# Filler matmuls in the setup of an attention and gated-MLP kernel, and a one-hot permute moved to ScalarE

## The chip, the cores and the metric

The kernel runs on one core of a Trainium2 chip. A core has five engines with instruction queues of their own: PE (TensorE, matrix products; its weight loads are listed apart as PEld), DVE (VectorE), ACT (ScalarE), POOL (GpSimd) and SP (SyncE, which here only issues transfers). Matmul results go to a small accumulation memory, PSUM, operands lie in SBUF, inputs and outputs in HBM, which DMA queues move. The metric is the device time of one execution in microseconds (us); smaller is better. The profile gives besides the span, from the first to the last instruction, and the clock that was granted to PE as a share of its full speed.

## The reference

Block-sparse attention over 4 batches of 8 heads, 768 positions of 64 dimensions, then a gated MLP whose gate mixes positions. A position block of 32 sees its neighbours, the first and last block, and three sampled blocks per row, which are an input.

```python
scores = scale * np.matmul(q, k.transpose(0, 1, 3, 2))
mask = np.abs(blk_i - blk_j) <= window
mask = mask | (blk_i == 0) | (blk_j == 0) | (blk_i == n_blocks - 1) | (blk_j == n_blocks - 1)
for qb in range(n_blocks):
    for kb in sampled_blocks[qb]:
        mask[qb * block:(qb + 1) * block, kb * block:(kb + 1) * block] = True
scores = np.where(mask, scores, -1000000000.0)
attn = softmax(scores)            # written out in the reference
x = (attn @ v), heads side by side: [4, 768, 512]

h = np.maximum(x @ w_in, 0.0)
u, v = halves of h
v_n = (v - mu) / np.sqrt(var + 1e-06)
v_s = np.einsum('ts,bsd->btd', w_spatial, v_n) + b_spatial[None, :, None]
out = (u * v_s) @ w_out
```

## The kernel before

The 32 (batch, head) units are walked in 16 pairs. The order of all instructions is written out by hand; the engines take theirs in program order, and a wait stops everything behind it on the same engine.

**The mask as extra rows.** The mask is not applied to the scores. Each key tile `kt` and query tile `qt` has 64 rows of data and 24 more: `kt` has the one-hot rows of the block of each position (`ind`), `qt` has the product of `bm` (0 where a block pair is allowed, a negative constant where it is not) with `ind`. So one matmul over 88 rows gives masked scores. `ind_nat` is made by POOL in natural order of positions (L157); `ind` is the same with the positions permuted to the order in which the data lies on the partitions (position 6p + c goes to column c*128 + p), a copy on POOL at L160.

**Setup.** SP and ACT issue the first loads: head 0 and head 1 of q and k in halves, then the rest. PE runs eight matmuls of 512 columns on a zero tile `warm` into a PSUM tile `wps` (L143 to L145) that nobody reads. DVE builds `allowed` from the sampled blocks with three operations (L172), then `bm` (L176), casts query head 0 (`nat_q`, L109), copies `ind` into `kt[0]` (L180). ACT casts key head 0 (`nat_k`, L107). Then PE transposes the keys (`tr_head`, L191, six transposes to PSUM), multiplies the mask rows (`mq`, L208), and transposes the queries (L191 again). DVE copies the transposed keys and queries out of PSUM (L183), ACT copies `mq` into `qt[0]` (L186). With that the first score tile can run.

**The main loop.** A step g handles one of the six 128-row key tiles of one head, 12 steps to a pair p. In a step, in this order: `qk_exp` (two score matmuls, L244, into one of two `sc` PSUM buffers, then one exponential on ACT, L248), in the first pairs preparation of later pairs, pieces of the MLP of an earlier batch, and, 7 steps behind, `av` (six matmuls against the values, L260), after six of which `norm` divides (L273, L274). For p = 0 there are also the copies of the mask rows to the other tiles (`mask_rows`, L215 and L216), head 1 of the pair (`second_head`, and `tr_head(1, ...)` at steps 3 and 4).

Pairs 1 to 4 are transposed on PE (`tr_pair`, L199); later ones by a transposing DMA on SP's queue (`tr_dma`, L227) out of the bf16 tiles that POOL casts (`prepare`, L109 and L112), and split by DVE (`split_pair`, L233). From pair 4 on the MLP of the batch before (L332 to L403) is spread over 48 steps; the last batch's MLP follows the loop. The attention output of every fourth pair is transposed on PE (`xtr`, L283), of the others by DMA (L287).

PSUM has four kinds of tiles, two buffers each where given: `moe` (transposes and MLP), `sc` (scores), `av` (value products).

Of the kernel before, what the change touches and what calls it, by code (L numbers as in the profile page):

```python
# [10 lines left out]
FP32 = mybir.dt.float32  # L11
BF16 = mybir.dt.bfloat16
I32 = mybir.dt.int32
AF = mybir.ActivationFunctionType
# [12 lines left out]
def kernel(  # L27
# [16 lines left out]
    nc = tc.nc  # L44

    B, H, S, D = q.shape
# [3 lines left out]
    NCH = S // 128  # L50
# [10 lines left out]
    KR = D + NB  # L61
# [3 lines left out]
    psum = ctx.enter_context(tc.tile_pool(name="psum", bufs=1, space=bass.MemoryType.PSUM))  # L65
# [3 lines left out]
    warm = const.tile([128, 512], BF16)  # L69
# [8 lines left out]
    kt = [const.tile([KR, S], BF16, name=f"kt{s}") for s in range(4)]  # L78
# [12 lines left out]
    def load(p, names="qkv", eng=nc.sync):  # L91
        b, g = divmod(p, NG)
        for nm, src in (("q", q), ("k", k), ("v", v)):
            if nm in names:
                eng.dma_start(out=st_tile(p, nm), in_=dram(src, b, 2 * g, 2))
# [7 lines left out]
    def cast_qk(p, nm, hs, eng):  # L103
        src = st[nm, p][:, hs].rearrange("p h (c d) -> p h c d", d=D)
        dst = nat[nm, p].rearrange("p c h d -> p h c d")[:, hs]
        if eng is nc.scalar:
            nc.scalar.activation(out=dst, in_=src, func=AF.Copy)  # L107
        else:
            eng.tensor_copy(out=dst, in_=src)  # L109

    def cast_v(p):
        nc.gpsimd.tensor_copy(  # L112
            out=vv[p % 3][:, :, :, 0:D],
            in_=st.pop(("v", p)).rearrange("p h (c d) -> p h c d", d=D))

    def prepare(p):
        for nm in "kq":
            nat_tile(p, nm)
            cast_qk(p, nm, slice(0, 2), nc.gpsimd)
        cast_v(p)  # L120
# [12 lines left out]
    ind_nat = const.tile([NB, S], BF16)  # L133
    ind = const.tile([NB, S], BF16)
# [5 lines left out]
    nc.vector.memset(tiny, 0.0)  # L140
    nc.scalar.activation(out=tiny, in_=tiny, func=AF.Exp)

    wps = psum.tile([128, 512], FP32, tag="moe", bufs=2)  # L143
    for _ in range(8):
        nc.tensor.matmul(out=wps, lhsT=warm[:, 0:128], rhs=warm, start=True, stop=True)  # L145


    colidx = const.tile([NB, NB], FP32)
# [8 lines left out]
    nc.gpsimd.affine_select(out=ind_nat, in_=ind_nat, compare_op=ALU.not_equal, fill=1.0,  # L157
                            base=0, pattern=[[-1, NB], [0, BLK]], channel_multiplier=1)
    make_identity(nc, ident)
    nc.gpsimd.tensor_copy(out=ind, in_=ind_nat.rearrange("b (p c) -> b c p", c=NCH))  # L160

    for s in range(3):
        nc.gpsimd.memset(vv[s][:, :, :, D:VA], 1.0)
# [13 lines left out]
                            op0=ALU.subtract, op1=ALU.mult)  # L177
    cast_qk(0, "q", slice(0, 1), nc.vector)
    cast_qk(0, "k", slice(0, 1), nc.scalar)
    nc.vector.tensor_copy(out=kt[0][D:KR, :], in_=ind)  # L180

    def dve_copy(o, i):
        nc.vector.tensor_copy(out=o, in_=i)  # L183

# [3 lines left out]
    def tr_head(h, nm, copy):  # L188
        ps = psum.tile([128, S], BF16, tag="moe", bufs=2)
        for c in range(NCH):  # L190
            nc.tensor.transpose(out=ps[0:D, c * 128:(c + 1) * 128], in_=nat[nm, 0][:, c, h],  # L191
                                identity=ident)
        copy((qt if nm == "q" else kt)[h][0:D, :], ps[0:D, :])
# [9 lines left out]
                                  in_=ps[h * D:(h + 1) * D, :])  # L203

    tr_head(0, "k", dve_copy)
    mq = psum.tile([128, 1024], FP32, tag="sc", bufs=2, name="mq")
    for hf in range(2):
        nc.tensor.matmul(out=mq[0:NB, hf * 512:hf * 512 + HALF], lhsT=bm,  # L208
                         rhs=ind[:, hf * HALF:(hf + 1) * HALF], start=True, stop=True)
    act_copy(qt[0][D:KR, :].rearrange("p (b c) -> p b c", b=2),  # L210
             mq[0:NB].rearrange("p (b c) -> p b c", b=2)[:, :, 0:HALF])
    tr_head(0, "q", dve_copy)

    def mask_rows(sl):
        nc.vector.tensor_copy(out=kt[sl][D:KR, :], in_=kt[0][D:KR, :])  # L215
        nc.vector.tensor_copy(out=qt[sl][D:KR, :], in_=qt[0][D:KR, :])  # L216

    def second_head():
        mask_rows(1)
        cast_qk(0, "k", slice(1, 2), nc.vector)  # L220
        cast_qk(0, "q", slice(1, 2), nc.vector)
# [3 lines left out]
    def tr_dma(p, nm):  # L225
        tt[nm, p] = work.tile([128, NCH, 128], BF16, tag=f"tt_{nm}", bufs=2, name=f"tt_{nm}")
        nc.sync.dma_start_transpose(out=tt[nm, p],  # L227
                                    in_=nat.pop((nm, p)).rearrange("p c h d -> p (c h d)"))
# [10 lines left out]
    def qk_exp(j, ci):  # L239
        if ci == 0:  # L240
            a_ref[j] = work.tile([128, NCH, S], BF16, tag="a_all", bufs=3, name="a_all")
        ps = psum.tile([128, 1024], FP32, tag="sc", bufs=2)
        for hf in range(2):
            nc.tensor.matmul(out=ps[:, hf * 512:hf * 512 + HALF],  # L244
                             lhsT=kt[j % 4][:, ci * 128:(ci + 1) * 128],
                             rhs=qt[j % 4][:, hf * HALF:(hf + 1) * HALF],
                             start=True, stop=True)
        nc.scalar.activation(  # L248
            out=a_ref[j][:, ci, :].rearrange("p (b c) -> p b c", b=2),
            in_=ps.rearrange("p (b c) -> p b c", b=2)[:, :, 0:HALF],  # L250
            func=AF.Exp, scale=0.125)

    def av(j, qc):
        if qc == 0:
            av_ref[j] = psum.tile([128, 512], FP32, tag="av", bufs=2,
                                  name="ps_av")[:, 0:NCH * VA].rearrange(
                                      "p (c d) -> p c d", d=VA)
        p, h = divmod(j, 2)
        for ci in range(NCH):
            nc.tensor.matmul(out=av_ref[j][:, qc, :],  # L260
                             lhsT=a_ref[j][:, ci, qc * 128:(qc + 1) * 128],
                             rhs=vv[p % 3][:, h, ci, :],
                             start=(ci == 0), stop=(ci == NCH - 1))
        if qc == NCH - 1:
            a_ref.pop(j)

    def norm(j):
        p, h = divmod(j, 2)
        if h == 0:
            xn_ref[p] = work.tile([128, NCH, 2, D], BF16, tag="xn", bufs=3, name="xn")  # L270
        ps = av_ref.pop(j)
        rc = work.tile([128, NCH, 1], FP32, tag="rc", bufs=2)
        nc.vector.reciprocal(out=rc, in_=ps[:, :, D:VA])  # L273
        nc.vector.tensor_tensor(out=xn_ref[p][:, :, h, :], in0=ps[:, :, 0:D],  # L274
                                in1=rc.to_broadcast([128, NCH, D]), op=ALU.mult)
# [138 lines left out]
    for p in range(NP + 1):  # L414
        for s in range(12):
            g = 12 * p + s
            j, ci = divmod(g, NCH)
            if p == NP and g - LAG >= 2 * NP * NCH:
                break
            if p < NP:  # L420
                qk_exp(j, ci)
            if p == 0 and s == 0:
                second_head()
            if p == 0 and s == 3:
                tr_head(1, "k", dve_copy)
            if p == 0 and s == 4:
                tr_head(1, "q", dve_copy)
                mask_rows(2)
                mask_rows(3)
            if p + 1 < NP and s in ((5, 9) if p else (7, 10)):  # L430
                (split_pair if p + 1 > NG else tr_pair)(p + 1, "k" if s < 9 else "q")
            if s == 10 and NG < p + 2 < NP:
                tr_dma(p + 2, "k")
                tr_dma(p + 2, "q")
            if p == 0 and s == 0:
                cast_v(0)
                prepare(1)
                load(2)
                nc.gpsimd.dma_start(out=ws_nat,
                                    in_=moe_w_spatial.rearrange("(p c) s -> p c s", c=NCH))  # L440
            if s == 7 and p + 2 < NP:
                if p + 3 < NP:
                    load(p + 3)
                prepare(p + 2)
                if p == 0:
                    nc.gpsimd.dma_start(out=w_in_t,
                                        in_=moe_w_in.rearrange("(g p) f -> p g f", p=128))
                if p == 1:
                    nc.gpsimd.dma_start(out=w_out_t,
                                        in_=moe_w_out.rearrange("(g p) f -> p g f", p=128))  # L450
            if moe_q and slots_left > 0:
                budget += sum(u[0] for u in moe_q) / slots_left
                slots_left -= 1
                while moe_q and budget >= moe_q[0][0] / 2:
                    ns, run = moe_q.popleft()
                    run()
                    budget -= ns
            if g >= LAG:
                ja, qc = divmod(g - LAG, NCH)
                av(ja, qc)  # L460
                if qc == NCH - 1:
                    norm(ja)
            if p in (2, 3) and s % 4 == 3:
                wspt_unit((p - 2) * 3 + s // 4)()
            if s == 8 and p >= 1:
                xtr(p - 1)
                if p % NG == 0:
                    moe_q.extend(moe_units(p // NG - 1))
                    slots_left = 48
                    budget = 0.0  # L470
# [35 lines left out]
```

## Time and profile before

| | us |
|---|---|
| median of 3 runs | 231.37 (231.24 to 231.6) |
| the profiled execution | 230.68 |
| its span | 228.9 |
| PE busy | 217.0 (95% of the span) |
| ACT busy | 171.3 (75%) |
| DVE busy | 131.9 (58%) |
| POOL busy | 52.8 (23%) |
| mean granted PE clock | 0.975 |

The profile page lists the busy time of each engine, the span in 40 slices, the DMA queues, the chain of work that ended last, and the costliest groups of instructions. [...] A few rows of the setup, from the instructions in order of time:

```profile
1.17 3.60 PE L145 MATMUL wps<-warm 128*128 128x512 bf16 x8 [1.17 <-DVE allowed L138]
...
3.46 1.65 DVE L172 SCALAR_TENSOR_TENSOR allowed<-colidx,samp_f,allowed 24x24 f32<-24x24 f32 x3
...
3.89 1.19 POOL L160 COPY ind<-ind_nat 24x768 bf16<-24x768 bf16 x1
...
4.70 0.85 PE L191 MATMUL ps<-ident,nat_k 128*64 128x128 bf16 x6
```

The columns are start, duration, engine, line, operation, output and inputs, count, and in brackets the idle time before and what ended it.

### The profile page before, as it was taken

The page shows a single profiled execution, that of the slowest core. Times are in us where ns is not written, and L with a number is a line of the kernel's source. Part 1 is how long each engine was busy: PE and PEld are TensorE (multiplying, and loading weights), DVE is VectorE, ACT ScalarE, POOL GpSimd, SP SyncE. Part 2 cuts the span into 40 slices and gives each one's busy share as a digit, 9 for nine tenths or more (in the row PEclk, how much of TensorE's full clock was granted, in tenths as well). Part 3 has the DMA queues.
Part 4 walks back from the last instruction along what each step waited for, and adds up shares of the span by engine and source line. Part 5 has one row for each costly group of instructions (what it writes and reads, how often), then busy time and mean ns, then how long its engine had stood idle before and what let it go on. Part 6 is the DMA issues. An engine that isn't in the chain of part 4 may idle for free.

```text
span 228.9 us, 5246 instructions
## 1 busy us (share of the span) xinstructions
PE 217.0 (95%) x2105; PEld 130.9 (57%) x2134; DVE 131.9 (58%) x285; ACT 171.3 (75%) x244; POOL 52.8 (23%) x83
## 2 busy tenths in 40 slices
PE   7799999999999999999999999999999999999993
PEld 3356677766566555665656555566656555544551
DVE  6643545647996545349995344269992423575532
ACT  3668999998799767786799666977798677256341
POOL 7440560421153401210172201210250000012000
PEclk9758999999999999999999999999999999999998
DMA  6589999999418273989838364999050423520015
GB/s 212 201 244 223 356 171 217 271 249 302 149 34 219 86 143 52 275 288 288 243 70 243 64 112 82 265 327 258 3 103 3 80 49 78 198 83 0 0 47 229
DMA packets 54940, 37.31 MB, mean 163 GB/s; under 512 B 38404, under 2 KB 51204, under 8 KB 54788
## 3 DMA queue, kind: packets, MB, share of 16 engines
q1 hardware_dynamic: 53428, 33.83, 54.7%
q0 software_dynamic: 1200, 2.75, 7.1%
q10 hardware_dynamic: 288, 0.39, 0.5%
q8 instruction: 16, 0.26, 0.5%
q14 instruction: 8, 0.07, 0.2%
HBM read 24.38 MB, written 6.29 MB: 134 GB/s over the span
## 4 chain that ended last, share of the span: by engine, by line
PE 76%; ACT 17%; DVE 2%; issue 2%; DMA 1%; ACTq 0%
PE ps L244 22%; ACT a_all L248 17%; PE ps_av L260 11%; PE ps_moe L377 10%; PE ps_moe L332 7%; PE ps_moe L395 7%; PE ps_moe L355 7%; PE ps_t L377 2%; PE ps_t L332 2%; PE ps_t L395 2%; PE ps_t L355 1%; PE ps_sc L377 1%; DMA samp_i<-in_sampled_blocks_dram 1%; PE ps_sc L355 1%; PE ps_sc L395 1%
## 5 line engine op out<-in xcount | busy, mean ns | idle before, releaser
L248 ACT ACTIVATE a_all<-ps 128x768 bf16<-128x768 f32 x192 | 144.2, 810 | 32.6 <-PE ps L244 32.0
L244 PE MATMUL ps<-qt,kt 88*128 88x384 bf16 x384 | 96.0, 332 | 5.2 <-ACT a_all L248 4.1
L260 PEld LDWEIGHTS <-a_all 128*128 128x128 bf16 x1152 | 62.0, 99 | 31.8 <-issue 0.7
L260 PE MATMUL ps_av<-vv,a_all 128*128 128x65 bf16 x1152 | 68.4, 195 | 0.0
L244 PEld LDWEIGHTS <-kt 88*128 88x128 bf16 x384 | 28.4, 99 | 11.0 <-issue 7.4
L380 DVE SCALAR_TENSOR_TENSOR gn<-ps_moe,b_col,un 128x512 bf16<-128x512 f32 x18 | 13.5, 751 | 27.6 <-PE ps_moe L377 27.6
L112 POOL CAST vv<-st_v 128x768 bf16<-128x768 f32 x16 | 13.6, 850 | 52.7 <-PE ps_av L260 43.1
L377 PE MATMUL ps_moe<-vn,w_spt 128*128 128x512 bf16 x99 | 24.8, 378 | 0.5
L377 PEld LDWEIGHTS <-w_spt 128*128 128x128 bf16 x144 | 13.8, 97 | 14.3
L345 POOL TENSOR_SCALAR std<-mv 128x3 f32<-128x3 f32 x8 | 1.9, 243 | 74.0 <-DVE mv L342 61.8
L109 POOL CAST nat_k<-st_k 128x768 bf16<-128x768 f32 x15 | 12.5, 836 | 27.3 <-issue 11.5
L274 DVE TENSOR_TENSOR xn<-ps_av,rc 128x384 bf16<-128x384 f32 x32 | 17.8, 557 | 1.4 <-DVE rc L273 0.3
L332 PE MATMUL ps_moe<-w_in_t,xt 128*128 128x512 bf16 x66 | 18.1, 378 | 0.3
L395 PE MATMUL ps_moe<-w_out_t,gt 128*128 128x512 bf16 x66 | 18.1, 378 | 0.3
L355 PE MATMUL ps_moe<-w_in_t,xt 128*128 128x512 bf16 x66 | 17.7, 378 | 0.3
L341 DVE BATCH_NORM_STATS2 stats<-vsb 128x6 f32<-128x512 bf16 x24 | 16.7, 694 | 1.9 <-ACT vsb L336 1.3
L332 PEld LDWEIGHTS <-xt 128*128 128x128 bf16 x96 | 9.3, 97 | 10.0 <-issue 0.7
L402 DVE COPY osb<-ps_moe 128x512 f32<-128x512 f32 x9 | 6.2, 692 | 15.0 <-PE ps_moe L395 14.9
L355 PEld LDWEIGHTS <-xt 128*128 128x128 bf16 x96 | 9.3, 97 | 9.5
L273 DVE RECIPROCAL rc<-ps_av 128x6 f32<-128x6 f32 x32 | 6.0, 186 | 13.4 <-PE ps_av L260 13.3
L395 PEld LDWEIGHTS <-gt 128*128 128x128 bf16 x96 | 8.9, 97 | 8.4
L359 DVE TENSOR_SCALAR vn<-vsb,mv,rstd 128x512 bf16<-128x512 bf16 x24 | 12.7, 564 | 0.6 <-POOL rstd L347 0.5
(85 smaller groups left out, 181.4 us busy)
## 6 DMA issues: line engine op xcount, KB each, us to landing
st_v<-in_v_dram SPq DMA_DIRECT2D x16, 384.0 KB, 6.2
out_dram<-osb SPq DMA_DIRECT2D x24, 256.0 KB, 2.3
st_q<-in_q_dram SPq DMA_DIRECT2D x15, 384.0 KB, 4.1
st_k<-in_k_dram SPq DMA_DIRECT2D x15, 384.0 KB, 4.7
ws_nat<-in_moe_w_spatial_dram POOLq DMA_DIRECT2D x1, 1152.0 KB, 12.5
w_in_t<-in_moe_w_in_dram POOLq DMA_DIRECT2D x1, 1024.0 KB, 11.8
w_out_t<-in_moe_w_out_dram POOLq DMA_DIRECT2D x1, 512.0 KB, 12.0
st_k<-in_k_dram ACTq DMA_DIRECT2D x2, 192.0 KB, 2.9
```

The lines of the kernel that those rows point to most:

```text
L112: nc.gpsimd.tensor_copy(out=vv[p % 3][:, :, :, 0:D], in_=st.pop(("v", p)).rearrange("p h (c d) -> p h c d", d=D))
L244: nc.tensor.matmul(out=ps[:, hf * 512:hf * 512 + HALF], lhsT=kt[j % 4][:, ci * 128:(ci + 1) * 128], rhs=qt[j % 4][:, hf * HALF:(hf + 1) * ...
L248: nc.scalar.activation(out=a_ref[j][:, ci, :].rearrange("p (b c) -> p b c", b=2), in_=ps.rearrange("p (b c) -> p b c", b=2)[:, :, 0:HALF], ...
L260: nc.tensor.matmul(out=av_ref[j][:, qc, :], lhsT=a_ref[j][:, ci, qc * 128:(qc + 1) * 128], rhs=vv[p % 3][:, h, ci, :], start=(ci == 0), st ...
L274: nc.vector.tensor_tensor(out=xn_ref[p][:, :, h, :], in0=ps[:, :, 0:D], in1=rc.to_broadcast([128, NCH, D]), op=ALU.mult)
L332: nc.tensor.matmul(out=ps, lhsT=xt(g)[:, tcc * 128:(tcc + 1) * 128], rhs=w_in_t[:, g, DH:DFF], start=(g == 0), stop=(g == NDM - 1))
L341: nc.vector.bn_stats(out=stats, in_=vsb[:, tcc, :])
L355: nc.tensor.matmul(out=ps, lhsT=xt(g)[:, tcc * 128:(tcc + 1) * 128], rhs=w_in_t[:, g, 0:DH], start=(g == 0), stop=(g == NDM - 1))
L359: nc.vector.tensor_scalar(out=vn[:, tcc, :], in0=vsb[:, tcc, :], scalar1=mv[:, tcc, 0:1], scalar2=rstd[:, tcc:tcc + 1], op0=ALU.subtract, ...
L377: nc.tensor.matmul(out=ps, lhsT=w_spt[:, sc, tcc * 128:(tcc + 1) * 128], rhs=vn[:, sc, :], start=(sc == 0), stop=(sc == NCH - 1))
L380: nc.vector.scalar_tensor_tensor(out=gn[:, tcc, :], in0=ps, scalar=b_col[:, tcc:tcc + 1], in1=un[:, tcc, :], op0=ALU.add, op1=ALU.mult)
L395: nc.tensor.matmul(out=ps, lhsT=gt[:, tcc, dhc, :], rhs=w_out_t[:, dhc, :], start=(dhc == 0), stop=(dhc == NDH - 1))
```

## The change

Four edits. `ind` is permuted by ACT (a Copy activation behind the key cast) and no longer by POOL. DVE's copy of `ind` into `kt[0]` goes behind its copy of the transposed keys. `wps` is taken from the `av` buffers, no longer from `moe`, and lives on through the setup, and a helper `keep_warm(n, cols)` issues n matmuls of the zero tile into it. It replaces the eight warm-up matmuls one for one, and stands at three new places: two of 128 columns before the mask product, six after the query transposes, and two in each of the first six steps of pair 0, after the score tile and ahead of `tr_head(1, ...)`. No new instruction has a wait of its own.

```diff
-    wps = psum.tile([128, 512], FP32, tag="moe", bufs=2)
-    for _ in range(8):
-        nc.tensor.matmul(out=wps, lhsT=warm[:, 0:128], rhs=warm, start=True, stop=True)
+    wps = psum.tile([128, 512], FP32, tag="av", bufs=2)
+
+    def keep_warm(n, cols):
+        for _ in range(n):
+            nc.tensor.matmul(out=wps[:, 0:cols], lhsT=warm[:, 0:128], rhs=warm[:, 0:cols],
+                             start=True, stop=True)
+
+    keep_warm(8, 512)
...
-    nc.gpsimd.tensor_copy(out=ind, in_=ind_nat.rearrange("b (p c) -> b c p", c=NCH))
...
-    nc.vector.tensor_copy(out=kt[0][D:KR, :], in_=ind)
-
+    nc.scalar.activation(out=ind, in_=ind_nat.rearrange("b (p c) -> b c p", c=NCH),
+                         func=AF.Copy)
...
     tr_head(0, "k", dve_copy)
+    nc.vector.tensor_copy(out=kt[0][D:KR, :], in_=ind)
+    keep_warm(2, 128)
...
     tr_head(0, "q", dve_copy)
+    keep_warm(6, 128)
...
             if p == 0 and s == 0:
                 second_head()
+            if p == 0 and s < 6:
+                keep_warm(2, 128)
             if p == 0 and s == 3:
                 tr_head(1, "k", dve_copy)
```

## The prediction

> **What bounds the kernel now.** I read first the page's slices, because the change is aimed at TensorE and its clock.
>
> ```profile
> span 228.9 us, 5246 instructions
> ...
> PE   7799999999999999999999999999999999999993
> ...
> PEclk9758999999999999999999999999999999999998
> ```
>
> PE is filled almost everywhere, but the granted clock (tenths of full speed; a slice is 5.7 us) sags to 7 and 5 in slices two and three and is back by slice four. That is one stretch. I then asked for PE's busy time in consecutive windows of 3.41 us, the spacing at which the clock changes (columns: window, length, busy time and count of PE, PEld, DVE, ACT, POOL, then clock, DMA share, GB/s).
>
> ```profile
> 2.17:5.59 3.42, 3.42 (x14) 1.32 (x12) 2.76 (x8) 1.47 (x3) 2.98 (x10) 1.00 1.02 331
> 5.59:9.00 3.41, 2.17 (x14) 0.96 (x13) 3.15 (x7) 2.16 (x3) 0.96 (x1) 1.00 0.92 314
> 9.00:12.41 3.41, 3.21 (x17) 1.58 (x17) 0.61 (x2) 2.47 (x4) 2.82 (x4) 0.50 0.16 40
> 12.41:15.83 3.42, 3.23 (x19) 1.66 (x18) 2.04 (x6) 2.34 (x3) 0.39 (x2) 0.50 1.01 330
> 15.83:19.24 3.41, 3.41 (x31) 2.53 (x30) 0.97 (x3) 2.44 (x3) 1.50 (x2) 0.50 0.99 197
> 19.24:22.65 3.41, 3.16 (x41) 2.10 (x39) 1.61 (x4) 2.97 (x5) 0.00 (x0) 1.00 0.97 226
> 22.65:26.07 3.42, 3.18 (x43) 2.33 (x43) 1.76 (x4) 3.33 (x5) 1.37 (x2) 1.00 1.03 379
> ```
>
> The window 5.59 to 9.00 is the only thin one: PE is busy 2.17 of 3.41 us. From 9.00 to 19.24, three windows, the clock is halved. The column to watch is ACT: 2.4 us of work per window in the cold stretch, 3.3 after it. What sets the end there is told by the chain of waits, in order of time:
>
> ```profile
> 4.00 1.13 DVE allowed L172
> ...
> 6.00 0.55 DVE kt L183
> 6.55 0.51 DVE qt L183
> 7.05 0.04 issue
> 7.10 0.51 PE ps L244 x2
> 7.61 0.02 issue
> 7.64 1.52 ACT a_all L248 x2
> ...
> 14.76 0.64 PE ps L199 x6
> 15.40 0.33 PE ps_av L260 x6
> 15.73 0.64 PE ps L244 x2
> ...
> 19.68 5.03 ACT a_all L248 x7
> ```
>
> DVE sets the start of the first score matmul (7.10). From 9.2 to 19.68 the chain is PE's matmuls at half clock; from 19.68 it is ACT's exponentials one behind the other, to about 53 us, and then PE with the MoE work to the end. The groups of ACT in the stretch 19.2 to 54 give the pace when PE isn't cold:
>
> ```profile
> L248 ACT ACTIVATE a_all<-ps 128x768 bf16<-128x768 f32 x47 | 34.3, 813 | 0.9 <-PE ps L244 0.5
> ```
>
> (34.3 + 0.9) / 47 = 0.749 us per exponential. Before that, the first starts at 7.64 and the twelfth at 19.68: 12.04 / 11 = 1.095 us each. The cold stretch costs 11 x (1.095 - 0.749) = 3.8 us.
>
> [...] only 1.00 and 0.50, a cold stretch of 10.24 us = 3 x 3.413, and six transposes of 128 columns take 0.64 us in the chain when cold and 0.34 when warm. [...] 9.00 to 12.41 was 3.21 us busy and stayed cold, and 1.70 us of it were transposes (L191). [...] two of the three L172 operations take 0.24 us, the third, beside POOL's 1.19 us copy of ind (3.89 to 5.08), 1.13.
>
> **The change part by part.**
>
> *One-hot permute off POOL.* The POOL copy goes; the third L172 should fall from 1.13 to 0.24 us and bm come 0.9 us earlier. It is worth about nothing: behind bm on DVE stands the nat_q cast, whose st_q half was issued at 1.23 and takes 3.0 to 4.0 us or more to land (so 4.2 to 5.2; it ran at 5.24), and PE is not free for the key transposes before its eight 512-column warm-up matmuls end; they stay, and the transposes start at 4.70 as now. ACT gets a 24x768 copy. The row of before does not show it; nearest are qt from PSUM, 0.80 us, and nat_k, 0.52 us for 384 elements. I take 0.8 (0.4 to 1.6 for the permuted reading): it runs after the nat_k cast (3.27 to 3.79), so 3.8 to 4.6, before its first reader, the mask matmul, at 5.5. ACT is idle until 6.04; queued behind it stands only the qt mask copy. Without that cover it would cost what goes beyond 5.5.
>
> *kt's mask rows after the key copy on DVE.* Order now: nat_q cast, kt from ind 0.35, kt from ps 0.55, qt from ps 0.55. The transposes end near 5.55. New: kt 5.58 to 6.13, ind rows to 6.49, qt 6.5 to 7.05. Same end, because the 0.35 only moves from before 0.55 to after it; bounds -0.1 to +0.1, I take 0.
>
> *Fillers.* Twenty 128-column weight load and matmul pairs: 2 + 6 in the setup, 2 after each of the six first score tiles. A pair of this size is 0.34 / 6 = 0.057 us warm and 0.64 / 6 = 0.107 us cold (the six-transpose rows of the chain). They wait for nothing; behind them on PE is the next real matmul, which waits.
> - Two before the mask matmul: cold, 0.21 us, at about 5.34 to 5.55, so the mask product ends near 6.1 in place of 6.0 and the ACT copy of it (0.80) near 6.9, before DVE's 7.05. Hidden by 0.15 us.
> - Six after the query transposes: 0.34 us, in PE's 0.65 us wait for DVE. Hidden; cold they would be 0.64, just hidden.
> - Two after each score tile: 0.114 us warm. A warm tile step on PE is 0.33 of scores + 0.114, against 0.749 of ACT; with a six-transpose group 0.79, absorbed by the two score buffers. Hidden while warm; cold 0.21 us each on PE's chain.
>
> *What they buy.* Streaming time by columns at full clock (my estimate: the 0.057 us of 128 columns scaled) in 5.59 to 9.00: before, mask 0.34, transposes 0.34, three score tiles 0.96: 1.64 us, 48%[...]; the clock fell. After: plus twelve fillers, 0.68: 2.32 us, 68%[...]. Next window, 9.0 to 12.4, warm: five tiles 1.6, six fillers 0.34, transposes 0.67: 76%[...]. From then on the steady pattern, scores 0.33 + value products 0.19 per 0.749: 69%, which held from 19.24 on. [...] I take it that the clock holds.
>
> *What is late next.* Twelve exponentials at 0.749 put the twelfth at 7.64 + 8.24 = 15.88: 3.8 us early, and all of ACT's chain with it, unless data is late. The transfers of the stretch run at DMA share 1.0 and do not move with the clock: vv for the third pair is cast at 24.70, needed near 34.3 - 3.8 = 30.5; nat_k of the fourth pair is cast by 27.72, needed at 32.47 - 3.8 = 28.7. The tight one is pair five:
>
> ```profile
> 42.68 0.83 POOL L109 CAST nat_k<-st_k 128x768 bf16<-128x768 f32 x1 [8.10 <-DMA st_k<-in_k_dram]
> ...
> 45.21 1.24 SPq L227 DMA_TRANSPOSE tt_k<-nat_k  x1
> ...
> 49.42 0.72 DVE L233 COPY kt<-tt_k 64x768 bf16<-64x768 bf16 x2 [1.20 <-DMA tt_k<-nat_k]
> ```
>
> POOL waits for st_k until 42.68 (issued at 28.96, behind other transfers), so the transposing DMA can go at 43.55 at the earliest, 1.7 us sooner than now and not 3.8. With 4.2 us to land and 0.72 of copies DVE is free at 48.5; its next work, rc at 51.42, would be due at 47.6. Late 0.85, of which 0.6 is slack (xn ends at 52.2, the transposes that read it start at 52.83). Loss 0 to 0.9; I take 0.2. After 54 us PE is the bound with under 3% idle, in a fixed order, and a shift stays.
>
> Sum: 0 + 0 + 0 - 3.8 + 0.2 = -3.6 us. Profiled execution 230.68 (span 228.9 and 1.8 around it) to 227.1, span 225.3. The three runs have the median 231.37, 0.7 above the profiled one; the same step gives 227.8.
>
> **The rivals.**
>
> A. The clock falls at 9.0 all the same. [...] Then the fillers after tiles four, five and six lie on a PE-bound chain: 2 to 3 x 0.21 = 0.4 to 0.64 us, and if the clock comes back at 19.24 as before, 231.9. [...] For it speaks that window 12.41 to 15.83, 3.23 us busy, did not regain the clock[...]. 0.17. If the fuller windows bring the clock back one window sooner, 3.41 / 0.97 cold steps against 3.41 / 0.749 is 1.0 step, 0.8 us: 231.1, no change. 0.07.
>
> B. Half the gain: the clock drops for one window (9.0 to 12.4 or the next), or the transfers of pair five take 1 us and more. One cold window costs the 0.8 us of above, with transposes in it 1.2; 229.0. For it: the DMA share of 1.0 throughout 13 to 50 us. 0.15.
>
> C. The fillers don't reach the array as activity, being zeros: no different from A in time. Against it: the eight zero matmuls of the start were followed by full clock at 5.59 (the six query transposes at 5.93 take 0.52 us, the six key transposes at 4.70 took 0.85). Its chance is inside A's.
>
> **How the numbers follow.** The clock holds: 0.60, 227.8, its own range 226.8 to 228.6 (gain 0.5 more if the unprofiled runs were cold for longer, 0.8 less by pair five). With B the range goes to 229.9. A and its variant are left outside, with 0.17 to 0.2. What a measurement can tell from no change is 0.2%, 0.46 us. Faster 0.76 (main, B, 0.01 from between), same 0.07, slower 0.17.
>
> **What would show it.** Right: clock 1.00 in all windows from 5.59; the twelfth exponential near 15.9; first score matmul still at 7.1; L172's third at 0.24 with no gain from it; PE's wait for DVE before the first score tile shortened by fillers; rc of the eighth head near 48.4 after a longer wait for tt_k. Wrong: 0.50 from 9.00, or from 12.4; score tiles that start well after the end of the exponential two before them, which frees their buffer; ACT waiting for PE near 50 us.

## The result and the profile after

The changed kernel takes 233.94 us (four runs, 232.99 to 234.81), the kernel before 231.49 us in the runs beside it: ratio 1.0104, 95% interval 1.0062 to 1.0147. It is slower by about 1%, where 1.6% faster was forecast. Ratios here and below are formed from undisturbed runs alone, so that one can differ from the ratio of two medians. The profiled execution took 233.79 us, with a span of 231.9 us, 3.0 us more than before.

The page of the changed kernel, its slices (one is 5.8 us):

```profile
span 231.9 us, 5286 instructions
...
PE   7999999976999999999999999999999999999993
...
PEclk9999999997999999999999999999999999999999
```

The sag of the clock at the start is gone from this row, and there is a new one in the tenth slice, with a dip of PE to 7 and 6 in slices nine and ten. Two things have to be looked at: what happened at the start, and what happened near 50 us. First the start, PE's first score tiles (L251) and ACT's exponentials (L255) in order of time (start, duration, engine, line, operation):

```profile
8.04 0.82 PE L251 MATMUL ps<-qt,kt 88*128 88x384 bf16 x2
...
10.61 0.48 PE L251 MATMUL ps<-qt,kt 88*128 88x384 bf16 x2
```

```profile
8.90 3.07 ACT L255 ACTIVATE a_all<-ps 128x768 bf16<-128x768 f32 x4 [1.45 <-PE ps L251]
...
12.13 0.81 ACT L255 ACTIVATE a_all<-ps 128x768 bf16<-128x768 f32 x1 [0.17 <-PE ps L251]
...
13.13 11.10 ACT L255 ACTIVATE a_all<-ps 128x768 bf16<-128x768 f32 x15 [0.19 <-PE ps L251]
```

The first tile comes at 8.04 and not at 7.10, and its two matmuls take 0.82 us (a pair took 0.80 to 0.83 in the kernel before at its recorded half clock); those at 10.61 take 0.48. So in this execution the full clock came late. The trace's record of clock changes has it at 10.03 us, where the profile before had it at 5.59. (Ahead of the first recorded change the clock column reads 1.00 whatever the matmuls show: the eight warm-up matmuls of 512 columns ran 0.43 us apart in both profiles; with the full clock on record, at 58.41 in this one, four of that size took 0.86 us, 0.22 each.) From then on ACT runs one exponential behind the other. The twelfth, the seventh of the last row, starts near 13.13 + 6 x 0.74 = 17.6 us; before, it was 19.68. The setup gained 2.1 us.

The new fillers of the setup have a part in the late first tile. In two profiles with a late clock and without them (two of the experiments below) it starts at 7.71; with them, here and in two more, at 8.04. The two in front of the mask product push that product from 5.48 to 5.80, and the query transposes and DVE's copy of the queries stand behind it.

Now the place where the gain is lost. The waits of PE over the whole execution, and PE's row there (columns of the first: engine, line, what it waited for, total, times, longest):

```profile
PE ps L290 <- DVE xn L281: 3.0, 1, 3.0
```

```profile
50.70 0.35 PE L267 MATMUL ps_av<-vv,a_all 128*128 128x65 bf16 x6
54.03 0.51 PE L290 MATMUL ps<-ident,xn 128*128 128x128 bf16 x6 [2.97 <-DVE xn L281]
```

These are the transposes of step eight of pair four. In the profile before:

```profile
52.47 0.36 PE L260 MATMUL ps_av<-vv,a_all 128*128 128x65 bf16 x6
52.67 0.50 PE L283 MATMUL ps<-ident,xn 128*128 128x128 bf16 x6
```

PE still leads by 1.8 us just ahead of them (50.70 against 52.47), so they should run near 50.9. They run at 54.03, 1.4 us later than before. What DVE did meanwhile:

```profile
45.59 0.56 DVE L281 TENSOR_TENSOR xn<-ps_av,rc 128x384 bf16<-128x384 f32 x1 [0.30 <-DVE rc L280]
52.55 0.72 DVE L240 COPY kt<-tt_k 64x768 bf16<-64x768 bf16 x2 [6.41 <-DMA tt_k<-nat_k]
53.20 0.18 DVE L280 RECIPROCAL rc<-ps_av 128x6 f32<-128x6 f32 x1
53.41 0.56 DVE L281 TENSOR_TENSOR xn<-ps_av,rc 128x384 bf16<-128x384 f32 x1
```

DVE stands 6.41 us in front of one copy: the transposed keys of pair five haven't landed. Behind it in DVE's queue lies the normalisation (rc, xn) that PE's transposes read. The keys themselves are not needed until pair five. Last, the windows at that place, in the spacing of the recorded clock changes, 3.41 us (columns as in the prediction):

```profile
47.57:50.99 3.42, 3.29 (x40) 2.17 (x39) 0.00 (x0) 3.42 (x6) 1.93 (x3) 1.00 1.39 122
50.99:54.40 3.41, 0.44 (x9) 0.38 (x8) 1.37 (x4) 0.74 (x2) 0.00 (x0) 1.00 1.20 245
54.40:57.82 3.42, 3.20 (x19) 1.64 (x18) 2.03 (x5) 0.81 (x1) 0.00 (x0) 0.50 1.18 299
57.82:61.23 3.41, 3.41 (x40) 2.06 (x38) 2.52 (x7) 2.85 (x4) 0.00 (x0) 1.00 0.92 314
```

PE is busy for 0.44 us of the second window, and in the third it runs at half clock. Here, with the MLP's matmuls on it, PE is the bound (busy 3.20 of 3.42 us). That is what the change set out to prevent, moved to another place: 1.4 us late from the stall, and 3.0 us late at the end.

### The profile page after: what moved, and what is told of

Same layout as the page of the kernel before. It is cut to its first block, busy times and chain, and to the rows that moved or that the text cites. A ratio compares the mean times of both kernels' runs of the same rounds, so it can differ in the third digit from the quotient of the medians.

```text
span 231.9 us, 5286 instructions
## 1 busy us (share of the span) xinstructions
PE 217.7 (94%) x2125; PEld 131.9 (57%) x2154; DVE 130.6 (56%) x285; ACT 172.1 (74%) x245; POOL 51.3 (22%) x82
## 4 chain that ended last, share of the span: by engine, by line
PE 77%; ACT 10%; DMA 5%; SPq 2%; issue 2%; DVE 1%; POOL 0%; POOLq 0%; ACTq 0%
PE ps L251 21%; PE ps_av L267 11%; ACT a_all L255 10%; PE ps_moe L384 10%; PE ps_moe L339 7%; PE ps_moe L402 7%; PE ps_moe L362 7%; DMA st_k<-in_k_dram 5%; PE ps_t L384 2%; PE wps L147 2%; PE ps_t L339 2%; PE ps_t L402 1%; PE ps_t L362 1%; PE ps_sc L384 1%; PE ps L195 1%
## 5 line engine op out<-in xcount | busy, mean ns | idle before, releaser
L255 ACT ACTIVATE a_all<-ps 128x768 bf16<-128x768 f32 x192 | 143.9, 810 | 35.4 <-PE ps L251 34.7
L251 PE MATMUL ps<-qt,kt 88*128 88x384 bf16 x384 | 95.1, 329 | 4.4 <-ACT a_all L255 3.5
L251 PEld LDWEIGHTS <-kt 88*128 88x128 bf16 x384 | 28.3, 98 | 8.9 <-issue 6.2
L339 PE MATMUL ps_moe<-w_in_t,xt 128*128 128x512 bf16 x66 | 18.9, 390 | 0.5 <-DMA st_k<-in_k_dram 0.2
L362 PE MATMUL ps_moe<-w_in_t,xt 128*128 128x512 bf16 x66 | 17.7, 378 | 0.3
L345 DVE TENSOR_SCALAR vsb<-ps_moe 128x512 bf16<-128x512 f32 x18 | 12.3, 682 | 2.4 <-PE ps_moe L339 2.4
```

Of the source, the lines that this page charges most:

```text
L251: nc.tensor.matmul(out=ps[:, hf * 512:hf * 512 + HALF], lhsT=kt[j % 4][:, ci * 128:(ci + 1) * 128], rhs=qt[j % 4][:, hf * HALF:(hf + 1) * ...
L255: nc.scalar.activation(out=a_ref[j][:, ci, :].rearrange("p (b c) -> p b c", b=2), in_=ps.rearrange("p (b c) -> p b c", b=2)[:, :, 0:HALF], ...
L339: nc.tensor.matmul(out=ps, lhsT=xt(g)[:, tcc * 128:(tcc + 1) * 128], rhs=w_in_t[:, g, DH:DFF], start=(g == 0), stop=(g == NDM - 1))
L362: nc.tensor.matmul(out=ps, lhsT=xt(g)[:, tcc * 128:(tcc + 1) * 128], rhs=w_in_t[:, g, 0:DH], start=(g == 0), stop=(g == NDM - 1))
```

## The experiments

**Without the new fillers.** Are the other edits to blame?

```diff
-    keep_warm(2, 128)
...
-    keep_warm(6, 128)
...
-            if p == 0 and s < 6:
-                keep_warm(2, 128)
```

> The changed kernel without its twenty new filler matmuls; the permute stays on ACT, the copy of ind behind the key copy. Theory 'late transfer' (the fillers bring the score tiles about 2 us forward, then PE waits 3 us for the transposed keys of pair five, and the clock drops once more): without fillers the clock is low from about 9 to 19 us as in the kernel before, no long wait of PE near 50 us, time within 0.4 us of the kernel before (231.1 to 231.9). Rival 'the other edits cost' (permute on ACT, or wps in the av buffers): still about 233 to 234.

Measured 231.74 us in twenty runs, ratio 1.0016 (0.9993 to 1.004). The permute on ACT, the copy order and the other PSUM tile cost nothing that can be seen (at most 0.4%). The loss comes with the fillers.

**Pair five transposed on PE.** The transposing DMA that DVE waits for is taken out of the kernel.

```diff
-                (split_pair if p + 1 > NG else tr_pair)(p + 1, "k" if s < 9 else "q")
+                (split_pair if p + 1 > NG + 1 else tr_pair)(p + 1, "k" if s < 9 else "q")
...
-            if s == 10 and NG < p + 2 < NP:
+            if s == 10 and NG + 1 < p + 2 < NP:
```

> The changed kernel, but pair five is transposed on PE like pairs one to four, not by DMA. 'Late transfer': PE's 3 us wait for xn near 51 us and the low clock at 54 to 58 us go, the 2 us of the setup reach the end less 0.7 us for twelve more transposes: span 227.5 to 229.5, time 229 to 231, below the kernel before. Rival 'fillers cost as such': 233 to 234 as the changed kernel.

Measured 228.68 us, ratio 0.9886 (0.9845 to 0.9926). PE's longest wait after the start is 0.5 us, and the clock is full from 5.38 us to the end. The fillers' gain is real, and the DMA of pair five is what took it.

**The same DMA sooner.** It stays, and the loads of pair six go behind it on SP.

```diff
                 tr_dma(p + 2, "q")
+                if p == 3:
+                    load(p + 3)
...
-                if p + 3 < NP:
+                if p + 3 < NP and p != 3:
                     load(p + 3)
```

> The changed kernel, with the loads of pair six issued on SP behind the transposing DMA of pair five, not ahead of it. If the transfer is late because 1.2 MB of loads stand before it in the queue: the transposed keys land 2 to 4 us sooner (by 49 us, not 52.5), PE's wait shrinks below 1 us, time 229 to 231. If it is late because an instruction fetch stalls the transposes: they start sooner, near 44 us, away from the fetch at 47.3 us, and the time is the same 229 to 231; if neither matters, 233 to 234.

Measured 227.90 us, ratio 0.9854 (0.9813 to 0.9894). DVE's rows in its profile:

```profile
47.41 0.72 DVE L240 COPY kt<-tt_k 64x768 bf16<-64x768 bf16 x2 [2.86 <-DMA tt_k<-nat_k]
48.06 0.20 DVE L280 RECIPROCAL rc<-ps_av 128x6 f32<-128x6 f32 x1
48.30 0.56 DVE L281 TENSOR_TENSOR xn<-ps_av,rc 128x384 bf16<-128x384 f32 x1
```

The keys land 5.1 us sooner than in the changed kernel, and xn is ready at 48.9 in place of 54.0. In this profile the clock was also full early, from 4.57 us on. Moving 1.2 MB of loads behind two transposes is enough.

**More PE instructions.** In the changed kernel the three transposing DMAs of this place were interrupted: between 47.9 and 49.3 us, and again from 50.4 to 50.9 and from 51.2 to 52.0, nearly no packet of theirs moved. A 16 KB instruction fetch of PE began at 47.33. Two fillers in each of the 24 steps of pairs zero and one bring that fetch forward and leave the queue order alone.

```diff
-            if p == 0 and s < 6:
+            if p < 2:
                 keep_warm(2, 128)
```

> The changed kernel, with two fillers in every one of the 24 steps of pairs zero and one, not in six. The 72 additional PE instructions bring PE's 16 KB instruction fetch about 3 us forward, to 44 us, before the transposes of 47.4 us; queue order and data stay. If the fetch stalls the transposes: keys of pair five land near 49.5 us and not 52.5, PE's wait falls from 3.0 to 0.5 us or less, time 230 to 231.5. If only the queue order matters: landing stays at 52 to 52.5 us, 233 to 234.

Measured 232.62 us (230.19 to 236.27 in twenty runs), ratio 1.0012 (0.9986 to 1.0039). The fetch moved to 45.21, the keys were copied at 51.12: neither the 49.5 of the one side nor the 52 to 52.5 of the other. PE's wait for xn fell to 1.3 us, not to 0.5. The first interruption was there again (47.3 to 48.6), with no fetch beside it, so it does not need one. Nor does it need the fillers: in the profile without them (the first experiment) the same three transposes were interrupted for 1.3 us too (45.5 to 46.8). What interrupts the transposes stays open. The clock fell here as well, from 52.98 to 56.39, after a window in which PE was busy for 2.01 of 3.42 us (49.56 to 52.98).

**The same reorder without fillers, and pair five on PE without fillers.** Is the reorder the gain by itself? Both are the kernel before with the diffs shown above.

> The kernel before, no fillers, with the loads of pair six issued behind the transposing DMA of pair five. Theory 'late transfer hides the setup gain': here the keys of pair five are not on the path (DVE waited 1.2 us for them, PE not at all), so moving them forward gains nothing: 231 to 231.9, low clock from 9 to 19 us. Rival 'the reorder itself is the gain, the fillers are not': 228 to 229.

> The kernel before, with pair five transposed on PE. Twelve more transposes of 0.057 us on a core that is bound by ACT until 53 us: 231.3 to 232.2 by the theory that the DMA is no limit there without the fillers; a gain (below 230.5) would say that the transposing DMA of pair five held the kernel before as well.

Measured 230.69 us, ratio 0.9986 (0.9962 to 1.0009), and 231.92 us, ratio 1.0042 (1.0027 to 1.0058). Without fillers neither gains. The second is slower by 0.4%, about what its twelve transposes would take (12 x 0.057 = 0.7 us, an estimate). The DMA of pair five is a limit only for a kernel that arrives there early.

**DVE asks later.** All transfers keep the order of the changed kernel. Only the two copies of pair five move in DVE's program, behind the normalisation.

```diff
-            if p + 1 < NP and s in ((5, 9) if p else (7, 10)):
-                (split_pair if p + 1 > NG else tr_pair)(p + 1, "k" if s < 9 else "q")
+            at = (9, 10) if p == NG else (5, 9) if p else (7, 10)
+            if p + 1 < NP and s in at:
+                (split_pair if p + 1 > NG else tr_pair)(p + 1, "k" if s == at[0] else "q")
```

> The changed kernel, all transfers in its order; only DVE's copies of pair five's transposed keys and queries are asked for later (steps nine and ten of pair four in place of five and nine), behind the normalisation and the copy that PE's transposes of step eight wait for. If PE stands still because the copy blocks DVE's queue and not because it needs the keys: keys still land at about 52 us, PE's 3 us wait for xn and the low clock at 54 us are gone, 228 to 230. If PE truly lacks the keys then: still 233 to 234.

Measured 229.52 us, ratio 0.9941 (0.9898 to 0.9983). Its DVE rows and three lines of PE's waits:

```profile
47.95 0.56 DVE L281 TENSOR_TENSOR xn<-ps_av,rc 128x384 bf16<-128x384 f32 x1
49.50 0.56 DVE L292 COPY xt<-ps 128x768 bf16<-128x768 bf16 x1 [0.99 <-PE ps L290]
51.28 0.74 DVE L240 COPY kt<-tt_k 64x768 bf16<-64x768 bf16 x2 [1.22 <-DMA tt_k<-nat_k]
```

```profile
PE ps L251 <- DVE qt L240: 0.5, 1, 0.5
PE ps_moe L339 <- DMA xt<-xn: 0.5, 1, 0.5
PE ps L290 <- DVE xn L281: 0.3, 1, 0.3
```

The keys are late still (51.28), and PE's wait falls from 3.0 to 0.3 us. PE stood still because a copy that nobody needed yet was first in DVE's queue. The transposes being late still costs something: the first two lines are waits that the kernel with the reordered loads does not have, for the queries of pair five and for another transposing DMA.

**Both.** The reordered loads and the later copies together.

> The changed kernel with both: pair six's loads behind pair five's transposing DMA, and DVE's copies of pair five asked for later. If the stall near 50 us is the whole of the loss, either of the two is enough and this one gives 227.3 to 228.5, equal within 0.5 us to the one with the reordered loads; if something of the stall remained there, up to 1 us less.

Measured 228.52 us, ratio 0.9905 (0.9874 to 0.9936). Nothing is added to the reorder alone: there is one stall, and either cure removes it. The later copies alone measured 1.0 us more than both together, with intervals that overlap; the two waits of 0.5 us above are gone in the profile of both.

**The stall filled.** How much of the loss is the stall, and how much the half clock behind it? The changed kernel, with twelve 512-column fillers where PE waits.

```diff
             if s == 8 and p >= 1:
+                if p == NG:
+                    hold = psum.tile([128, 512], FP32, tag="moe", bufs=2, name="hold")
+                    for _ in range(12):
+                        nc.tensor.matmul(out=hold, lhsT=warm[:, 0:128], rhs=warm,
+                                         start=True, stop=True)
                 xtr(p - 1)
```

> The changed kernel with twelve 512-column fillers on PE ahead of the transposes of step eight of pair four, the place where PE stands still for 3 us. The transfer and DVE's wait stay. If the loss is made of the stall (1.4 us against the kernel before) and of one window at half clock after it (1.6 us): the clock stays full near 54 to 58 us and the time falls by 1 to 1.6 us, to 232 to 233. If the half clock costs nothing there, because PE isn't the bound: 233.5 to 234.5.

Measured 231.62 us in twenty runs, ratio 1.0022 (1.0003 to 1.004). The place in its profile, and the window behind it:

```profile
51.11 2.54 PE L478 MATMUL hold<-warm 128*128 128x512 bf16 x11
...
54.27 0.51 PE L290 MATMUL ps<-ident,xn 128*128 128x128 bf16 x6 [0.63 <-DVE xn L281]
```

```profile
54.40:57.90 3.50, 3.50 (x38) 2.15 (x37) 2.73 (x6) 2.18 (x3) 0.00 (x0) 1.00 1.17 298
```

The transposes run no sooner (54.27), the clock stays full, and the profiled execution takes 232.71 us, 1.1 less than that of the changed kernel; the medians, from different sets, differ by 2.3. I put the half clock after the stall at 1.1 to 2.3 us of the loss, an estimate from these two differences, beside the 1.4 us of the stall itself.

**Which fillers hold the clock.** The best version so far once more, and beside it one with only the twelve fillers behind the score tiles, and one with only the eight of the setup (the other calls of the helper are left out).

> The same kernel as the one with pair six's loads behind pair five's transposing DMA, beside the kernels of this set on one chip: 227.5 to 229, 0.98 to 0.99 of the kernel before.

> That kernel without the eight setup fillers (two before the mask product, six before the first score tile); the twelve after the score tiles stay. [...] the gap of 0.6 us before the first tile is empty again[...], the clock falls in a part of the runs, 228 to 231, wider spread. If the twelve suffice: 227.5 to 229 as with all twenty.

> That kernel with the eight setup fillers and without the twelve after the score tiles. Two to three score tiles of 0.33 us with gaps of 0.4 us remain in the window after the setup: about 45% streaming, the clock falls for two or three windows, 230 to 231.5. If the setup fillers suffice: 227.5 to 229.

| | runs | us |
|---|---|---|
| all twenty | 4 | 227.62, 227.68, 228.26, 229.17 |
| twelve behind the tiles | 22 | ten from 227.34 to 229.46, twelve from 230.98 to 234.16 |
| eight in the setup | 4 | 228.28, 232.16, 232.37, 234.65 |

With all twenty: 227.97 us, ratio 0.9871 (0.982 to 0.9922), which repeats the 227.90. With a part of them the times fall in two groups, the better one as good as with all. The profile of the eight-filler version is one of the second group; ACT's first exponentials in it:

```profile
8.89 1.51 ACT L255 ACTIVATE a_all<-ps 128x768 bf16<-128x768 f32 x2 [1.45 <-PE ps L251]
...
12.82 0.81 ACT L255 ACTIVATE a_all<-ps 128x768 bf16<-128x768 f32 x1 [0.72 <-PE ps L251]
```

The first exponential is at 8.89 and the fifth 3.93 us later, at 12.82; with the clock full, in the version with all twenty, it is 3.08 us (7.46 to 10.54). PE's score matmuls take 0.80 to 0.85 us a pair from 8.65 to 15.22, as in the kernel before at its recorded half clock (0.80 to 0.83), and the record has the full one only from 20.18. My expectation for it, that the clock would rise and fall again, was wrong in kind: in this execution it came only after 20 us. The profile of the version with twelve is of the second group too, with the full clock from 17.40. So the better group is probably the executions in which the clock comes early; none of them was profiled. One program has both groups, ten and twelve of 22 executions: what parts them differs between executions.

## Why the prediction was wrong

**The other edits: right.** The three L172 operations take 0.76 us together (1.65 before), and nothing was gained from it; the permute took 1.22 us on ACT (0.8 taken, 1.6 the upper end) and ended at 4.88, before its reader at 5.80. The run without fillers confirms that all this is worth nothing.

**The clock holds: right, and the gain of 3.8 us to within 0.5, where the clock is on time.** In the reordered version the clock record starts at 4.57 us and ACT's rows are

```profile
7.46 2.92 ACT L255 ACTIVATE a_all<-ps 128x768 bf16<-128x768 f32 x4 [0.80 <-PE ps L251]
...
11.54 8.80 ACT L255 ACTIVATE a_all<-ps 128x768 bf16<-128x768 f32 x12 [0.19 <-PE ps L251]
```

so that the twelfth exponential starts near 11.54 + 6 x 0.733 = 15.9, against 15.88 predicted and 19.68 before (16.1 in the repeat of this kernel, 16.3 in the one with pair five on PE). In the profiled execution of the changed kernel only 2.1 us of it were there, because the full clock came at 10.03. "First score matmul still at 7.1" held only where it came early. With a late clock the two fillers before the mask product were not "hidden by 0.15" either: they cost 0.33 us (8.04 against 7.71), because the sum followed the mask product to ACT and not the query transposes behind it to DVE. That fuller windows would hold the clock was my estimate: in the reordered version PE was busy for 3.20 and 2.97 of 3.41 us from 4.57 on, at 1.00; how full a window has to be was not shown. And the sum took its start from one profile, that of the kernel before. The runs show a start that differs: first full clock at 4.57, 4.90, 5.38 and 5.59 us in some profiles, at 10.03 and 10.54 in others, and at 17.40, 20.18 and 20.63 in three without all of the fillers. The net loss is not explained by this: by 50.7 us the changed kernel was ahead of the kernel before, and the stall decided the rest.

**What is late next: the step that failed.** The right place was named, with the sentence "the transposing DMA can go at 43.55 at the earliest, 1.7 us sooner than now", and DVE was to be free at 48.5, at a loss of 0 to 0.9 us, 0.2 taken. DVE was free at 53.3. Three things were wrong in it.

First, an issue was taken for a start. The load of pair five landed a little later than before (POOL cast nat_k at 43.22, not 42.68). SP did issue the transposing DMA sooner (44.31 against 45.21), behind these rows of the changed kernel:

```profile
39.08 1.10 SPq L95 DMA_DIRECT2D st_q<-in_q_dram  x1
40.23 0.46 SPq L95 DMA_DIRECT2D st_k<-in_k_dram  x1
40.78 1.03 SPq L95 DMA_DIRECT2D st_v<-in_v_dram  x1
41.91 2.31 SPq L294 DMA_TRANSPOSE xt<-xn  x1
44.31 1.92 SPq L234 DMA_TRANSPOSE tt_k<-nat_k  x1
46.33 3.21 SPq L234 DMA_TRANSPOSE tt_q<-nat_q  x1
```

Pair six's loads are ahead of it. In the packet records of the trace the first 256-byte packets (the transposes) of this group move at 47.41 us, in the kernel before at 47.42: not sooner by anything. The reorder shows that this can be moved, by 4.8 us (42.62).

Second, the duration to landing was taken over from before: 4.2 us there, 8.2 here. Of the difference 0.9 us is the wait in the queue, entered sooner, and 3.1 us lie behind the first packet, where the interruptions are. The group of three transposes took from 47.42 to 50.74 before, and from 47.41 to 52.54 in the changed kernel. From its first packet to the landing of the keys it was 2.0 us before, 5.1 in the changed kernel, and 3.5 in the version without the new fillers (45.01 to 48.49): the one profile of before gave a duration that did not repeat. DVE was free 4.8 us later than forecast: 1.7 us of it is the first point, 3.1 us is this one. The range of 0 to 0.9 us left no room for either.

Third, lateness was priced at its own length. PE was busy for 0.44 of 3.41 us, and the next 3.42 us, where it is the bound, were at half clock. In the run with more PE instructions the same followed on a wait of 1.3 us (PE busy 2.01 of 3.42 us). The half clock added 1.1 to 2.3 us by the estimate above (the run with the stall filled). The prediction had the same sequence from the setup (2.17 of 3.41 us busy, then half clock from 9.00 to 19.24) and didn't apply it here.

**The rivals.** B said that transfers of pair five could take 1 us and more, with 229.0; it was the right mechanism at a third of its size (PE waited 3.0 us), and I had it end below the kernel before. A, the clock falling in spite of the fillers at 9.0, is not what happened in the profiled execution. In the two profiles with only part of the fillers the full clock came late, and that isn't A either. The rival that loses should have been built on the DMA share of 1.0 that stood in the windows shown: the stage that moved forward (PE 1.8 us ahead at 50.7) came before its data, and DVE stood 6.41 us in front of them.

## What to carry to other kernels

When a stage is sped up, list what each engine's queue will then wait for first, and ask whether that wait is for something needed now: an early copy at the head of an in-order queue turned a late transfer into a 3 us stop of PE, though PE did not read its data until pair five. For the transposes here the time of issue said little (issued 0.9 us sooner, first packet at 47.41 against 47.42); with the loads queued behind them and not ahead, the first packet came at 42.62, and ordering the urgent transfer first gave the best version here (227.9 us, 1.3 to 1.5% below the kernel before and 2.6% below the changed one). And fillers that are to keep the clock have to be placed for the waits that the change creates, too: those of the setup did not cover the 3.0 us wait near 51 us, and half clock followed it (54.40 to 57.82).

## What the runs showed of the hardware

The recorded clock differs between executions of one program: the mean clock of the kernel without the new fillers was 0.978 in ten of its twenty executions and 1.00 in three. The recorded stretches at half clock inside the kernels last 10.24 us (9.00 to 19.24 in the kernel before) or 3.41 us (54.40 to 57.82 in the changed one, 52.98 to 56.39 with more PE instructions). In the windows of 3.41 us just ahead of these stretches PE was busy for 2.17 us (before), 0.44 (changed) and 2.01 (more PE instructions). In all other windows of the first two at recorded full clock, up to 224 us, it was busy for 2.87 us or more.

A mean clock can mislead: one profile of the reordered kernel without fillers has a mean of 0.997 though the record has no full clock until 20.6 us. Three of its exponentials start 0.97 us apart ahead of that (17.35, 18.32, 19.29), as in the kernel before at its recorded half clock (16.41, 17.38, 18.35). Ahead of the first recorded change the column reads 1.00, as it does from 4 to 15 us in the profile with eight fillers.

The version with twelve fillers has two groups of times, 227.34 to 229.46 and 230.98 to 234.16 us. With twelve matmuls on zeros of 512 columns in the stall the clock stood at 1.00 in the window behind it, and at 0.50 without them.

A transposing DMA of 768 packets took 0.7 us with no packets beside it but 4-byte ones of its own queue (48.12 to 48.82 in the kernel before), and 9 us (30.19 to 39.00) while casting loads of the MLP weights ran on POOL's queue, with about as many packets of the one as of the other (234 and 222 between 33 and 36 us).
